# Five chunks held back for the third-stage stretch in a long convolution with a gated mix

## The chip, the cores and the metric

The kernel runs on one core of a Trainium2 chip. The time is device microseconds (us) of one launch. Five engines work side by side, each on its own queue of instructions, in the order in which they were written: TensorE (PE, matmuls; PEld is its weight load), VectorE (DVE), ScalarE (ACT), GpSimd (POOL), and SyncE (SP), which issues the DMAs here. An instruction waits at the head of its queue until what it needs is there, and everything behind it on that engine waits with it. Matmuls write to PSUM, which the kernel holds as a few buffers that are used in turn.

## The reference

```python
Xf = np.fft.rfft(x, n=2 * S, axis=1)           # x: 8 x 6400 x 128
Hf = np.fft.rfft(h, n=2 * S, axis=0)           # h: 6400 x 128
y = np.fft.irfft(Xf * Hf[None], n=2 * S, axis=1)[:, :S]
gate_pre[:, s] = sum_k conv_w[k] * y[:, s - 4 + k]     # 5 taps, zeros before the start
out = (1 / (1 + np.exp(-gate_pre)) * (y @ w_val)) @ w_out
```

A convolution as long as the sequence, per channel, through a transform; then a five-tap convolution along the sequence gives a gate for a projection, and the gated result is projected again. Everything is float32.

## The kernel before

The transform of length 6400 is split as 100 x 64 and done with matmuls by constant matrices, in four stages for each of the 8 batches.

- The *first stage* (`Forward`): GpSimd makes a difference and a sum of two halves of the input (`sums`, tiles `sd` from tiles `x`), PE multiplies them by the matrix `r1` (`half`), ScalarE copies the result into `gy`.
- The *second stage* (`Product`): for each of 13 blocks `kb`, PE multiplies `gy` by a block of the matrix `m2` that is loaded anew each time (three buffers); VectorE multiplies the result by the spectrum of `h`, in two instructions (`mul_u` writes back to `gy`, `mul_t` into the buffer of `h` itself), and GpSimd joins the two with two adds. The spectrum is loaded too, into four buffers `h`. Each of these loads is 512 KB.
- The *third stage* (`s3_quads`): 16 steps. PE multiplies `gy` by `r3` into a pair buffer of PSUM; ScalarE copies a part to one of the `h` buffers and writes the ends, VectorE makes two joins into the large tile `dt`.
- The *fourth stage* (`Chunk.s4`): 13 chunks of positions, twelve of five and one of four (`HEAD`, positions 60 to 63). PE multiplies a slice of `dt` by the resident matrix `m4`. ScalarE copies the chunk (`copies`: the values `y`, the initial value of the gate's cells, and a scaled copy `q` for one tap), VectorE adds the other taps in three instructions or a few more (`taps`), GpSimd adds `q`. Then PE projects `y` (`project`), ScalarE takes the sigmoid (`sigm`), VectorE multiplies (`gate`), PE projects again (`output`), ScalarE copies and SP stores (`store`).

The program alternates between two stretches. In the **third-stage stretch** of a batch each of the 16 steps holds one third-stage step and one half of the next batch's first stage, and after these some of the last batch's deferred work. In the **fourth-stage stretch** that follows, each step holds one chunk of the fourth stage, one product of the next batch, and the projections of earlier chunks. Five chunks, those at positions 35 to 55, are *late*: in the fourth stretch only their values are copied; their taps, gate and projections come in the next third stretch, two steps for each. They have tiles of their own (`yl`, and `gl` for the cells). All other chunks keep values and cells in `dt`.

The order is written out by hand: the dictionary `steps` places deferred work in the third stretch, `jobs` places projections in the fourth, and a wrapper keeps every engine in program order. PSUM has two pair buffers (third stage, products) and four single ones (first and fourth stage, projections). A chunk's single buffer is free when its taps have been read from it.

Of the kernel before, what the change touches and what calls it, by code (L numbers as in the profile page):

```python
# [36 lines left out]
DEFER = 35  # L37
# [4 lines left out]
XH = 8  # L42

# [78 lines left out]
def longconv_moe(ctx: ExitStack, tc: tile.TileContext, x, h, r1, m2, r3, m4, w64, out):  # L122
# [23 lines left out]
    m2_sb = [cp.tile([128, SB, 2, C], F32, name=f"m2_{i}") for i in range(M2B)]  # L146
    h_sb = [cp.tile([128, 2 * SB * C], F32, name=f"h_{i}") for i in range(HB)]
    x_sb = [cp.tile([128, 2, XG, N2], F32, name=f"x_{i}") for i in range(XB)]
    sd_sb = [cp.tile([128, 2, XG, N2], F32, name=f"sd_{i}") for i in range(3)]
    p_t = [cp.tile([128, CH, N1], F32, name=f"p_{i}") for i in range(2)]  # L150
    hd = dp.tile([NKB, 128, 2 * SB * C], F32, name="hd")
# [241 lines left out]
    def cells(x, n):  # L393

        out, i = [], 0
        while i < n:
            y = x + i
            end = 4 if y < 4 else LATE if y < LATE else N2
            k = min(n - i, end - y)
            s = (y - 4) % N2  # L400
            out.append((i, gl[:, y - LATE : y - LATE + k] if y >= LATE else dv[:, s : s + k, 1, :N1]))
            i += k
        return out

    class Chunk:


        def __init__(self, b, ch, defer):
            self.b, self.ch = b, ch
            a, n = ch  # L410
            self.late = defer and DEFER <= a < HEAD[0]
            self.y = yl[a][:, :n] if a >= LATE else dv[:, a : a + n, 0, :N1]
# [26 lines left out]
        def copies(self):  # L439
# [8 lines left out]
            else:  # L448
                act(self.y, self.p)
                if not self.late:  # L450
                    self.init()
                    self.q = p_t[a // CH % 2]
                    self.first(3, self.q, self.p)
            if self.late:
                self.p = self.y

# [5 lines left out]
        def taps(self, js=range(4)):  # L462
            a, n = self.ch
            if self.late and 0 in js:
                self.init()
                self.q = p_t[a // CH % 2]
                self.first(3, self.q, self.p)
# [15 lines left out]
            if 3 not in js:  # L483
                return
            for i, o in cells(a + 3, n):
# [68 lines left out]
    m4_rest = [12, 11, 10, 9, 4, 8, 5, 7, 6]  # L554
# [24 lines left out]
    for b in range(B):  # L579
# [4 lines left out]
        for m, c in enumerate(pend[1:]):  # L584
            steps[2 * m] += [lambda c=c: c.taps(range(2))]
            steps[2 * m + 1] += [lambda c=c: c.taps(range(2, 4))]
            steps[2 * m + 2] += [c.project, c.sigm, c.gate]
            if m < 3:
                steps[2 * m + 4] += [c.output]
                steps[2 * m + 5] += [c.store]  # L590
        if pend:
            steps[13] += [pend[0].project, pend[0].sigm, pend[0].gate]
# [3 lines left out]
        for g in range(NS):  # L596
# [14 lines left out]
            if nxt and g % 2 and g > 1:  # L611
                kb = g // 2 - 1
                if kb < M2B:
                    m2_load(kb)
                elif kb < M2B + HB - 1:
                    h_load(kb - M2B)
# [8 lines left out]
        cs = [Chunk(b, ch, nxt) for ch in CHUNKS]  # L625
        jobs = collections.defaultdict(list)
        for i, c in enumerate(cs):
            if i and not c.late:
                jobs[i + 2 if nxt else (5, 6, 7, 8, 9, 10, 11, 11, 12, 13, 13, 14)[i - 1]].append(c)
        if not nxt:  # L630
            jobs[NCH + 1].append(cs[0])
        ps, outs = {}, []
        for s in range(max(NCH - 1, *jobs) + 2):
            if s < 2:
                cs[s].s4()
            if s == 0 and pend:
                pend[0].output()
                pend[0].store(p_t[1][:, : HEAD[1]])
            if nxt and s == 0:
                ps[0] = Product(0)  # L640
                m2_load(M2B)
            if nxt and s + 1 < NKB:
                ps[s + 1] = Product(s + 1)
                m2_load(s + 1 + M2B)
# [6 lines left out]
            late = pend[4 + s : 5 + s] if s < 2 else []  # L651
# [66 lines left out]
```

## Time and profile before

| what | value |
|---|---|
| median of 3 runs (lowest to highest) | 1002.31 us (1001.48 to 1006.22) |
| profiled execution, its span | 1004.56 us, 1002.7 us |
| PE, DVE busy | 871.8 us (87%), 745.1 us (74%) |
| POOL, ACT busy | 570.1 us (57%), 509.6 us (51%) |
| moved by DMA | 177.40 MB, 177 GB/s on average |

Third- and fourth-stage stretches lie one behind the other from 97.6 us on; before that the spectrum of `h` is made and batch 0 goes through its first two stages. An average over the whole span mixes the two kinds of stretch, so the views are read stretch by stretch: from the first matmul of the third stage (`pt<-r_sb,gy`) to the first of the fourth (`pt<-m_sb,dt`) and on to the next batch's third. All program lines appear under the line of one helper, L109, so instructions are told apart by their tiles and shapes. In the rows, "pt" is a PSUM buffer, and the words in brackets say how long the engine was idle before and who ended the wait.

### The profile page before, as it was taken

What the parts mean: (1) busy time and instruction counts of PE and PEld (TensorE: products, weight loads), DVE (VectorE), ACT (ScalarE), POOL (GpSimd) and SP (SyncE); (2) the same over time, 40 slices, a digit from 0 to 9 for tenths busy, and PEclk for the clock granted to TensorE, in tenths of its full rate; (3) what the DMA queues carried; (4) which work ended last, traced back from release to release, by engine and by line L of the source; (5) the groups of instructions that cost most, each with busy time, mean ns of one, the idle gap of its engine ahead of it and who ended that gap; (6) DMA issues with size and microseconds to landing.
All of it is one profiled execution on the core that took longest, in us unless ns stands there. A gap on an engine that the chain in (4) does not pass through costs nothing. (4 is left out here: it accounts for less than half of the span.)

```text
span 1002.7 us, 47817 instructions
## 1 busy us (share of the span) xinstructions
PE 871.8 (87%) x21360; PEld 719.6 (72%) x21360; DVE 745.1 (74%) x1033; ACT 509.6 (51%) x1207; POOL 570.1 (57%) x586
## 2 busy tenths in 40 slices
PE   7898769988799879988899778988799888997778
PEld 6798668775688558775788657876688757884554
DVE  5556547968598767968499675968589675978666
ACT  4431444546553654547444663546544574545456
POOL 5457535775477754786277663776367762761032
PEclk9799879999999989999899999999899999999999
DMA  7684647846486456855486565855478454850103
GB/s 255 229 304 190 192 141 258 262 107 185 154 264 185 144 160 213 231 135 164 142 264 183 141 197 162 242 157 162 134 240 222 139 170 138 266 144 23 42 22 111
DMA packets 96844, 177.40 MB, mean 177 GB/s; under 512 B 43392, under 2 KB 49792, under 8 KB 96640
## 3 DMA queue, kind: packets, MB, share of 16 engines
q1 hardware_dynamic: 96640, 174.35, 56.2%
q8 instruction: 168, 2.75, 1.1%
q14 instruction: 36, 0.29, 0.1%
HBM read 141.56 MB, written 32.77 MB: 174 GB/s over the span
## 5 line engine op out<-in xcount | busy, mean ns | idle before, releaser
L109 POOL TENSOR_TENSOR gy<-gy,h 128x512 f32<-128x512 f32 (+1 forms) x182 | 221.2, 1242 | 120.1 <-PE pt L109 87.5
L109 PEld LDWEIGHTS pt<-r_sb,gy 64*64 64x64 f32 x8192 | 157.1, 145 | 103.6 <-issue 60.6
L109 DVE TENSOR_TENSOR dt<-pt,h 128x496 f32<-128x496 f32 x256 | 159.7, 664 | 96.2 <-ACT dt L109 91.8
L109 PEld LDWEIGHTS pt<-m_sb,dt 128*64 128x64 f32 x4096 | 194.0, 139 | 51.2 <-issue 34.2
L109 PE MATMUL pt<-r_sb,gy 64*64 64x64 f32 x8192 | 173.6, 233 | 60.1 <-issue 45.2
L109 PE MATMUL pt<-m_sb,dt 128*64 128x100 f32 x4096 | 200.2, 253 | 14.5 <-DVE dt L109 13.0
L109 POOL TENSOR_TENSOR sd<-x 128x256 f32<-128x256 f32 x236 | 182.0, 803 | 47.1 <-issue 21.2
L109 PEld LDWEIGHTS pt<-gy,m 128*64 128x64 f32 x3008 | 179.8, 135 | 27.7 <-issue 22.8
L109 PE MATMUL pt<-r_sb,sd 50*64 50x100 f32 x4608 | 155.0, 270 | 46.0 <-issue 21.0
L109 PE MATMUL pt<-gy,m 128*64 128x128 f32 x3008 | 190.8, 277 | 0.6 <-PE pt L109 0.5
L109 PEld LDWEIGHTS pt<-r_sb,sd 50*64 50x64 f32 x4608 | 128.6, 149 | 55.1 <-issue 24.2
L109 ACT COPY dt<-pt 128x16 f32<-128x16 f32 (+3 forms) x397 | 113.8, 329 | 103.6 <-PE pt L109 103.6
L109 DVE TENSOR_TENSOR gy<-pt,h 128x1024 f32<-128x1024 f32 (+1 forms) x99 | 116.7, 1179 | 58.3 <-ACT gl L109 34.4
L109 DVE SCALAR_TENSOR_TENSOR dt<-pt,w_sb,dt 128x500 f32<-128x500 f32 (+7 forms) x216 | 132.5, 629 | 10.6 <-POOL dt L109 6.7
L109 ACT COPY gy<-pt 128x400 f32<-128x400 f32 x248 | 112.2, 512 | 42.5 <-PE pt L109 31.2
L109 ACT COPY h<-pt 128x512 f32<-128x512 f32 (+1 forms) x136 | 83.5, 614 | 91.5 <-issue 43.0
L109 POOL TENSOR_TENSOR gl<-gl,p 128x500 f32<-128x500 f32 (+1 forms) x48 | 56.8, 1183 | 114.4 <-DVE gl L109 94.0
L109 PE MATMUL pt<-dt,w_sb 128*64 128x500 f32 (+2 forms) x480 | 115.1, 555 | 2.4 <-ACT dt L109 1.8
L109 DVE SCALAR_TENSOR_TENSOR gl<-yl,w_sb,gl 128x500 f32<-128x500 f32 (+1 forms) x112 | 106.1, 953 | 13.4 <-ACT gl L109 12.1
L109 DVE TENSOR_TENSOR h<-pt,h 128x1024 f32<-128x1024 f32 (+1 forms) x91 | 107.7, 1183 | 3.1
L109 ACT COPY yl<-pt 128x500 f32<-128x500 f32 (+1 forms) x89 | 51.3, 577 | 91.8 <-PE pt L109 91.7
L109 POOL TENSOR_TENSOR dt<-dt,p 128x500 f32<-128x500 f32 (+1 forms) x64 | 66.3, 1041 | 23.2 <-PE pt L109 13.2
(44 smaller groups left out, 657.6 us busy)
## 6 DMA issues: line engine op xcount, KB each, us to landing
m<-m SPq DMA_DIRECT2D x90, 512.0 KB, 5.4
h<-hd SPq DMA_DIRECT2D x84, 512.0 KB, 5.1
x<-xl SPq DMA_DIRECT2D x118, 256.0 KB, 2.9
out<-dt SPq DMA_DIRECT2D x56, 250.0 KB, 4.4
out<-yl SPq DMA_DIRECT2D x40, 250.0 KB, 4.6
m_sb<-m SPq DMA_DIRECT2D x12, 375.0 KB, 5.9
hd<-h SPq DMA_DIRECT2D x8, 512.0 KB, 4.9
m_sb<-m SPq DMA_DIRECT2D x6, 512.0 KB, 7.2
```

The costliest lines, as they stand in the source:

```text
L109: return self._tc.keep_in_program_order(call(*args, **kwargs))
```

## The change

The chunks at 10 to 30 become *held*: in the fourth stretch their taps are added as before, but their projection, sigmoid, gate and output come in the steps 0 to 6 of the next third stretch (stores up to step 7). The late chunks move back there by four steps, to steps 4 to 14, and one more of their outputs is done there instead of in the fourth stretch. To have a place until then, values and cells of positions 10 to 34 leave `dt` for a tile `ring`, which also takes the place of the three `m2` and four `h` buffers: in the first half of the fourth stretch it holds those, in the second the held chunks. So the products come earlier: two in even steps, one in odd ones, all 13 within nine steps. The fourth stage takes `HEAD`, 0, then the late chunks, then 5 to 30. The first loads of `m2` and `h` for the next batch stand at steps given by a table, `AHEAD`. GpSimd's add of `q` is taken out of `taps` and comes one step later, after the next chunk's taps; `q` then needs four buffers instead of two, and two of them are `sd` tiles. Cells of a chunk that crosses position 10 are two pieces instead of one. The five loads of `m4` blocks that are left for batch 0's fourth stretch come in another order, and its 17 steps in batch 7 follow the same rule, projection three steps behind the chunk.

```diff
-DEFER = 35
+HELD = 10
+BL = 2 * SB * C
+AHEAD = {2: (1, 0), 7: (0, 0), 9: (0, 1), 10: (0, 2), 11: (1, 1), 13: (1, 2)}
...
+    ring = cp.tile([128, (M2B + HB) * BL], F32, name="ring")
+    ring_at = [ring[:, i * BL : (i + 1) * BL] for i in range(M2B + HB)]
+    m2_sb = [r.rearrange("p (s a c) -> p s a c", a=2, c=C) for r in ring_at[:M2B]]
+    h_sb = [ring_at[M2B + i] for i in (2, 0, 1, 3)]
+    held_c = ring[:, : (LATE - HELD) * N1].rearrange("p (n t) -> p n t", t=N1)
...
+            self.held = defer and HELD <= a < LATE
+            self.y = yl[a][:, :n] if a >= LATE else held_y[a] if a >= HELD else dv[:, a : a + n, 0, :N1]
...
+        def keep(self):
+            self.q = p_t[self.i % 2] if self.late else keeps[self.i % 4]
+            self.first(3, self.q, self.p)
...
-            if 3 not in js:
-                return
-            for i, o in cells(a + 3, n):
+        def add(self):
+            for i, o in cells(self.ch[0] + 3, self.ch[1]):
                 nc.gpsimd.tensor_tensor(out=o, in0=o, in1=self.q[:, i : i + o.shape[1]], op=ADD)
...
+        for c in pend:
+            a = c.ch[0]
+            if a == HEAD[0]:
+                t = NS - 1
+            elif c.held:
+                t = (a - HELD) // CH
+            else:
+                t = 6 + 2 * (a - LATE) // CH
+                steps[t - 2] += [lambda c=c: c.taps(range(2))]
+                steps[t - 1] += [lambda c=c: c.taps(range(2, 4)), c.add]
+            steps[t] += [c.project, c.sigm, c.gate]
+            if t + 2 < NS:
+                steps[t + 2] += [c.output]
+                steps[t + 3] += [c.store]
...
+            kbs = list(range(at, min(at + 2 - s % 2, NKB))) if nxt else []
+            at += len(kbs)
             if s < 2:
                 cs[s].s4()
...
+            if s == 0:
+                s2(0)
+            for kb in kbs[:1]:
+                s2(kb + 1)
...
             if 1 < s < NCH:
                 cs[s].s4()
...
+            for kb in kbs[:1]:
+                times(kb)
+            for kb in kbs[1:]:
+                s2(kb + 1)
             if s < NCH:
                 cs[s].copies()
...
+            for kb in kbs[1:]:
+                times(kb)
             if 0 < s <= NCH and not cs[s - 1].late:
                 cs[s - 1].taps()
+            if 2 < s < NCH + 2 and not cs[s - 2].late:
+                cs[s - 2].add()
             for c in jobs[s]:
                 c.gate()
```

Here `s2(kb)` issues a product's matmuls and the load of the block of `m2` three further on, `times(kb)` the multiplications, the adds and the load of the block of `h` four further on.

PE, second half of a middle batch's fourth stretch, up to the first matmuls of the third stage (`pt<-r_sb,gy`). `m_sb,dt` is a chunk's fourth stage, `gy,m` or `gy,ring` a product, `dt,w_sb` a projection or an output. Before:

```order
L109 MATMUL pt_8198<-gy,m_1_81 64x64x2 x16
L109 MATMUL pt_8215<-dt,w_sb 64x500 x2
L109 MATMUL pt_8218<-m_sb,dt 64x2x50 x20
L109 MATMUL pt_8239<-dt,w_sb 64x500 x2
L109 MATMUL pt_8251<-gy,m_2_82 64x64x2 x16
L109 MATMUL pt_8268<-m_sb,dt 64x2x50 x20
L109 MATMUL pt_8289<-dt,w_sb 64x500 x2
L109 MATMUL pt_8302<-gy,m_0_80 64x64x2 x8
L109 MATMUL pt_8311<-m_sb,dt 64x2x50 x20
L109 MATMUL pt_8337<-m_sb,dt 64x2x50 x20
L109 MATMUL pt_8369<-r_sb,gy 64x64 x32
```

And now:

```order
L111 MATMUL pt_6340<-gy,ring 64x64x2 x8
L111 MATMUL pt_6349<-m_sb,dt 64x2x50 x20
L111 MATMUL pt_6378<-m_sb,dt 64x2x50 x20
L111 MATMUL pt_6411<-m_sb,dt 64x2x50 x20
L111 MATMUL pt_6440<-dt,w_sb 64x500 x2
L111 MATMUL pt_6443<-m_sb,dt 64x2x50 x20
L111 MATMUL pt_6476<-m_sb,dt 64x2x50 x20
L111 MATMUL pt_6497<-dt,w_sb 64x500 x2
L111 MATMUL pt_6509<-m_sb,dt 64x2x50 x20
L111 MATMUL pt_6552<-r_sb,gy 64x64 x32
```

The last product now stands six chunks ahead of the third stage, and of the projections only one chunk's are left there.

VectorE in the same place. `gy<-pt` and the row after it are a product, SCALAR_TENSOR_TENSOR are taps, `dt<-pt,h` or `dt<-pt,ring` the joins of the third stage. Before:

```order
L109 TENSOR_TENSOR dt<-pt_8215,dt 128x5x100
L109 TENSOR_TENSOR gy<-pt_8198,h_85 128x2x64x8
L109 TENSOR_TENSOR h_85<-pt_8198,h_85 128x1024
L109 TENSOR_TENSOR gy<-pt_8251,h_86 128x2x64x8
L109 TENSOR_TENSOR h_86<-pt_8251,h_86 128x1024
L109 TENSOR_TENSOR gy<-pt_8302,h_83 128x2x64x4
L109 TENSOR_TENSOR h_83<-pt_8302,h_83 128x512
L109 TENSOR_TENSOR dt<-pt_8369,h_86 128x124x4
```

And now:

```order
L111 SCALAR_TENSOR_TENSOR ring<-pt_6443,w_sb,ring 128x500 x3
L111 SCALAR_TENSOR_TENSOR ring<-pt_6476,w_sb,ring 128x500 x3
L111 SCALAR_TENSOR_TENSOR ring<-pt_6509,w_sb,ring 128x500
L111 SCALAR_TENSOR_TENSOR ring<-pt_6509,w_sb,ring 128x400
L111 SCALAR_TENSOR_TENSOR gl<-pt_6509,w_sb,gl 128x100
L111 SCALAR_TENSOR_TENSOR ring<-pt_6509,w_sb,ring 128x300
L111 SCALAR_TENSOR_TENSOR gl<-pt_6509,w_sb,gl 128x200
L111 TENSOR_TENSOR dt<-pt_6552,ring 128x124x4
L111 TENSOR_TENSOR dt<-pt_6552,ring 128x62x2x4
L111 TENSOR_TENSOR ring<-pt_6613,ring 128x500
```

Where products stood ahead of the first joins there are now taps, and the gate of a held chunk (the last row) stands behind the first two joins.

GpSimd in the same place. `gy<-gy` are a product's adds, `ring<-ring` and `gl<-gl` the adds of `q`, `sd<-x` the sums of the first stage. Before:

```order
L109 TENSOR_TENSOR gl<-gl,p_93 128x300
L109 TENSOR_TENSOR gy<-gy,h_84 128x64x8 x2
L109 TENSOR_TENSOR gy<-gy,h_85 128x64x8 x2
L109 TENSOR_TENSOR gy<-gy,h_86 128x64x8 x2
L109 TENSOR_TENSOR gy<-gy,h_83 128x64x4 x2
L109 TENSOR_TENSOR sd_90<-x_87 128x256 x2
```

And now:

```order
L111 TENSOR_TENSOR ring<-ring,sd_85 128x500
L111 TENSOR_TENSOR ring<-ring,p_87 128x500
L111 TENSOR_TENSOR ring<-ring,p_88 128x500
L111 TENSOR_TENSOR ring<-ring,sd_84 128x200
L111 TENSOR_TENSOR gl<-gl,sd_84 128x300
L111 TENSOR_TENSOR sd_84<-x_81 128x256 x2
```

The adds of the last held chunks now stand ahead of the first sums; the last product's adds are far ahead of them.

More of the change, by code (lines that the diff above doesn't have):

```diff
@@ L397, in cells @@
             y = x + i
-            end = 4 if y < 4 else LATE if y < LATE else N2
+            end = next(e for e in (4, HELD, LATE, N2) if y < e)
             k = min(n - i, end - y)
             s = (y - 4) % N2
-            out.append((i, gl[:, y - LATE : y - LATE + k] if y >= LATE else dv[:, s : s + k, 1, :N1]))
+            t, o = (gl, y - LATE) if y >= LATE else (held_c, y - HELD) if y >= HELD else (dv[:, :, 1, :N1], s)
+            out.append((i, t[:, o : o + k]))
             i += k
@@ L465, in taps @@
                 self.init()
-                self.q = p_t[a // CH % 2]
-                self.first(3, self.q, self.p)
+                self.keep()
             if a == HEAD[0]:
@@ L583, in longconv_moe @@
         steps = collections.defaultdict(list)
[L584 to L592, printed above, removed]
+        for c in pend:
[12 more added lines that the diff above has]
+                steps[t + 3] += [c.store]
+        pend = [c for c in pend if c.ch[0] in (HEAD[0], HEAD[0] - CH)]
         if nxt:
@@ L610, in longconv_moe @@
                     m4_load(m4_rest.pop(0))
[L611 to L616, printed above, removed]
+            if nxt and g in AHEAD:
+                f, kb = AHEAD[g]
+                (h_load if f else m2_load)(kb)
             for u in steps[g]:
@@ L622, in longconv_moe, with s2, times @@
             fx = Forward(x[b + 2], gy)
-        cs = [Chunk(b, ch, nxt) for ch in CHUNKS]
+        chs = CHUNKS if not nxt else sorted(CHUNKS, key=lambda c: (c != HEAD, c[0] > 0, c[0] < LATE))
+        cs = [Chunk(b, i, ch, nxt) for i, ch in enumerate(chs)]
         jobs = collections.defaultdict(list)
         for i, c in enumerate(cs):
-            if i and not c.late:
-                jobs[i + 2 if nxt else (5, 6, 7, 8, 9, 10, 11, 11, 12, 13, 13, 14)[i - 1]].append(c)
+            if i and not c.late and not c.held:
+                jobs[i + 3].append(c)
         if not nxt:
-            jobs[NCH + 1].append(cs[0])
-        ps, outs = {}, []
-        for s in range(max(NCH - 1, *jobs) + 2):
+            jobs[NCH + 2].append(cs[0])
+        pr = {}
+        def s2(kb):
+            if nxt and kb < NKB:
+                pr[kb] = Product(kb)
+                m2_load(kb + M2B)
+        def times(kb):
+            if kb in pr:
+                pr[kb].mul_u()
+                pr[kb].mul_t()
+                pr.pop(kb).add()
+                h_load(kb + HB)
+        outs, at = [], 0
+        for s in range(max(NCH, *jobs) + 2):
+            kbs = list(range(at, min(at + 2 - s % 2, NKB))) if nxt else []
+            at += len(kbs)
             if s < 2:
                 cs[s].s4()
[L636 to L644, printed above, removed]
+            late = pend[s : s + 1]
+            if late and s == 0:
+                late[0].output()
+                late[0].store(p_t[1][:, : HEAD[1]])
+                late = []
+            if s == 0:
+                s2(0)
+            for kb in kbs[:1]:
+                s2(kb + 1)
             if m4_rest:
@@ L671, in longconv_moe @@
                 fx.load(XB)
-        pend = [cs[0]] + [c for c in cs if c.late]
+        pend = [cs[0]] + [c for c in cs if c.held or c.late]
 def _lay_x(v):
```

25 lines of the change are left out of this document (10 added, 15 removed).

## The prediction

> **What bounds the kernel now.** I read the page's busy shares first, then the windows of the alternating stretches (columns: window, its length, then busy time and instruction count of PE, PEld, DVE, ACT, POOL; granted clock; DMA share; GB/s). The third-stage stretch of batch 0 starts at 97.6, its fourth-stage stretch at 153.4, and so on to the two of batch 7.
>
> ```profile
> PE 871.8 (87%) x21360; PEld 719.6 (72%) x21360; DVE 745.1 (74%) x1033; ACT 509.6 (51%) x1207; POOL 570.1 (57%) x586
> ...
> 97.60:153.40 55.80, 37.93 (x1536) 36.38 (x1537) 30.17 (x55) 25.30 (x80) 24.10 (x33) 0.80 0.46 150
> ...
> 265.20:324.50 59.30, 59.26 (x984) 50.63 (x984) 51.19 (x66) 25.70 (x47) 40.50 (x36) 1.00 0.74 217
> 324.50:380.80 56.30, 43.92 (x1576) 32.81 (x1573) 38.45 (x54) 34.55 (x100) 30.98 (x37) 0.91 0.46 143
> ...
> 840.40:899.70 59.30, 59.30 (x988) 50.59 (x988) 51.18 (x66) 25.71 (x47) 40.51 (x36) 1.00 0.70 213
> 899.70:942.10 42.40, 28.84 (x1064) 20.07 (x1062) 33.66 (x54) 21.92 (x68) 6.24 (x5) 1.00 0.06 22
> 942.10:1002.70 60.60, 50.87 (x632) 32.38 (x632) 37.22 (x62) 36.76 (x70) 15.46 (x15) 0.94 0.22 67
> ```
>
> A fourth-stage stretch is PE's: 59.26 busy of 59.30, VectorE close behind with 51.2. A third-stage stretch belongs to no engine: PE 43.9 and VectorE 38.5 of 56.3. One period (fourth stretch, then the next batch's third) takes (840.4 − 153.4) / 6 = 114.5 us. The timeline shows how a third stretch starts and how the fourth after it does:
>
> ```profile
> 324.55 1.19 PE L109 MATMUL pt<-r_sb,gy 64*64 64x64 f32 x64
> 326.96 0.92 PE L109 MATMUL pt<-r_sb,sd 50*64 50x100 f32 x32 [1.23 <-POOL sd L109]
> 327.70 1.14 PE L109 MATMUL pt<-r_sb,gy 64*64 64x64 f32 x64
> ...
> 329.35 1.14 PE L109 MATMUL pt<-r_sb,gy 64*64 64x64 f32 x64
> ...
> 380.82 1.59 PE L109 MATMUL pt<-m_sb,dt 128*64 128x100 f32 x32 [0.55 <-DVE dt L109]
> ...
> 385.04 1.22 DVE L109 TENSOR_TENSOR gy<-pt,h 128x1024 f32<-128x1024 f32 x1 [4.37 <-ACT gl L109]
> ```
>
> Step 0 already waits 1.23 us for GpSimd's sums (sd), so step 1 starts 3.15 after step 0. A step that nothing holds takes PE 1.65 (327.70 to 329.35). VectorE's first product comes 4.2 after the fourth stretch begins (380.82 to 385.04).
>
> **The change, part by part.** Prices are start-to-start times in one step of a fourth stretch:
>
> ```profile
> 404.15 2.28 DVE L109 SCALAR_TENSOR_TENSOR dt<-pt,w_sb,dt 128x500 f32<-128x500 f32 x3
> ...
> 405.06 2.01 PE L109 MATMUL pt<-gy,m 128*64 128x128 f32 x32
> ...
> 406.35 0.67 DVE L109 TENSOR_TENSOR dt<-pt,dt 128x500 f32<-128x500 f32 x1
> ...
> 406.86 1.26 POOL L109 TENSOR_TENSOR dt<-dt,p 128x500 f32<-128x500 f32 x1
> 406.90 1.01 PE L109 MATMUL pt<-dt,w_sb 128*64 128x500 f32 x4
> 406.93 1.21 DVE L109 TENSOR_TENSOR gy<-pt,h 128x1024 f32<-128x1024 f32 x1
> ...
> 407.74 1.89 PE L109 MATMUL pt<-m_sb,dt 128*64 128x100 f32 x40
> ...
> 408.18 1.22 DVE L109 TENSOR_TENSOR h<-pt,h 128x1024 f32<-128x1024 f32 x1
> ...
> 409.32 2.28 DVE L109 SCALAR_TENSOR_TENSOR dt<-pt,w_sb,dt 128x500 f32<-128x500 f32 x3
> ...
> 409.47 1.00 PE L109 MATMUL pt<-dt,w_sb 128*64 128x500 f32 x4
> 409.53 2.52 POOL L109 TENSOR_TENSOR gy<-gy,h 128x512 f32<-128x512 f32 x2 [1.42 <-PE pt L109]
> ```
>
> PE: a product 1.84 (405.06 to 406.90), a projection or an output about 0.8 (406.90 to 407.74), a chunk's fourth stage 1.73. VectorE: a product 2.4 (406.93 to 409.32), a chunk's taps 2.2 (404.15 to 406.35), a gate 0.6. GpSimd: a product's two adds 2.52, a chunk's add 1.26.
>
> *Leaving the fourth stretch*: five projections, five outputs and one late output (of the chunk at 50), 11 × 0.8 = 8.8 us of PE, and five gates of 0.67, 3.4 us of VectorE. Cell ranges now also break at position 10, which adds two short taps (+0.6). So PE needs 59.3 − 8.8 = 50.5 and VectorE 51.2 − 3.4 + 0.6 = 48.4. If all of it vanished into PE's idle time of the third stretch, 8.8 a period would be won. I choose otherwise, because the order is no longer mixed: thirteen products stand in the first nine steps and six chunks' taps behind them, with no product beside them.
>
> *The fourth stretch.* VectorE waits 4.2 for its first product. In steps 5, 6 and 7 the next product's matmuls (1.84) stand on PE behind a chunk's fourth stage (1.73), once also behind an output; with two pair buffers VectorE waits about 1.2 in each, 3.5 in all, and some 1.4 in the tail (the gate of the chunk at 5 behind its late add and sigmoid). Its last tap ends at 4.2 + 48.4 + 4.9 = 57.5 after the stretch began. PE has only 10 us of matmuls beside those last 14.7 us of taps (6 × 2.25 and a gate) and reaches the first quads of the third stage at about 53.
>
> *The add one block behind.* The add of a chunk now waits for the next chunk's taps, so the last two (chunks at 25 and 30; the latter in two pieces) run after the last tap: about 2.5. Only then come the sums that the forward stage wants, on the same queue.
>
> ```profile
> L109 POOL TENSOR_TENSOR sd<-x 128x256 f32<-128x256 f32 x236 | 182.0, 803 | 47.1 <-issue 21.2
> ```
>
> Two of 0.80: the first forward half starts at 57.5 + 2.5 + 1.6 = 61.6, and with it (0.7) and the held projection (0.8) step 1 starts at 63.1. Before, it started at 59.3 + 3.15 = 62.5. What PE saved is given back as one idle gap, 54 to 61.6; queued behind it are step 1's quads, and VectorE stands with the gate of the chunk at 10 ahead of step 1's joins.
>
> *The third stretch.* Steps 1 to 3 have no late taps: PE's 1.65 plus 0.8, 1.6 and 1.6 of held work, 8.9; VectorE (two joins, a gate) and ScalarE have less. A gap costs the clock besides. The rows are two PE gaps and windows at and after them:
>
> ```profile
> 366.04 1.86 PE L109 MATMUL pt<-r_sb,gy 64*64 64x64 f32 x57 [2.19 <-issue]
> ...
> 372.04 0.64 PE L109 MATMUL pt<-r_sb,gy 64*64 64x64 f32 x26 [2.11 <-issue]
> ...
> 365.00:369.00 4.00, 2.96 (x93) 2.96 (x97) 1.11 (x3) 1.20 (x5) 2.52 (x4) 0.63 0.76 264
> ...
> 373.00:377.00 4.00, 4.00 (x103) 2.53 (x100) 1.83 (x3) 1.87 (x6) 0.00 (x0) 0.59 0.02 4
> ```
>
> After such a gap the granted clock was 0.63 and 0.59 over 4 us: 1.5 us of PE time lost. For a gap of 7.6 I take 2.0 (bounds 0 and two such windows, 3.0). The Trainium skill ("TensorE: Matmul & The Clock Gate", Part 1, the HAM clock gate) says the array drops to half rate after an idle window of about 3.4 us and returns after a busy one. By that rule the gap surely spans a window, and half rate lasts 3.4 to 6.8 us, 1.7 to 3.4 of PE time; the trace shows the drop after shorter gaps than the rule asks.
>
> Steps 4 and 5 hold the first late chunk. From its add on, pairs of steps follow one another in a closed chain:
>
> ```profile
> 570.29 1.26 POOL L109 TENSOR_TENSOR gl<-gl,p 128x500 f32<-128x500 f32 x1 [2.49 <-DVE gl L109]
> ...
> 572.84 2.43 DVE L109 SCALAR_TENSOR_TENSOR gl<-yl,w_sb,gl 128x500 f32<-128x500 f32 x2
> ...
> 575.19 1.24 DVE L109 TENSOR_TENSOR dt<-pt,h 128x496 f32<-128x496 f32 x2
> ...
> 577.23 1.26 POOL L109 TENSOR_TENSOR gl<-gl,p 128x500 f32<-128x500 f32 x1 [2.49 <-PE pt L109]
> ```
>
> Add, sigmoid, gate, two taps, joins, tap, add: 6.94 a pair. The change leaves that chain as it is: four pairs, 27.8. Up to the first add, steps 4 and 5 take quads 1.1, ScalarE's copies about 1.1, joins 1.24, the held gate 0.67, and 4.4 from the two taps to the add (572.84 to 577.23): 8.5, and I add 0.7 for an issue gap. The held outputs and stores (up to step 7) lie in its slack. Two steps remain after the last add, 55.8 / 16 = 3.5 each (batch 0's stretch, which has no late work).
>
> *Sum of a period*: 63.1 + 8.9 + 2.0 + 8.5 + 0.7 + 27.8 + 7.0 = 118.0, against 114.5: +3.5, six times, +21.
>
> *The other stretches.* Batch 0 loads five blocks of constants (375 KB each, 1.9 MB) in the first steps, beside products that now come two to a step. What loads cost, and the fastest 4 us of them:
>
> ```profile
> m<-m SPq DMA_DIRECT2D x90, 512.0 KB, 5.4
> h<-hd SPq DMA_DIRECT2D x84, 512.0 KB, 5.1
> ...
> 277.00:281.00 4.00, 4.00 (x85) 4.00 (x82) 3.96 (x9) 1.02 (x3) 2.33 (x3) 1.00 1.02 358
> ```
>
> At 358 GB/s the blocks take 5.3; I charge 2, since not every load is late (bounds 0 and 5.3). In the other batches a product needs two of these loads, 1.05 MB or 2.9 us at that rate, where products come every 3.0 us on average: just covered. An h buffer turns round in a product (2.4), its adds (2.52) and a landing (5.1), 10.0 for four products: covered as well.
>
> Batch 7 has no forward stage, so no sums are waited for; its third stretch is the late chain alone, 6.0 a pair (first two rows, of the chain of waits). Its fourth stretch runs taps, add, taps, add in series, 3.74 a chunk (last two rows):
>
> ```profile
> 906.36 1.26 POOL gl L109
> ...
> 912.37 1.25 POOL gl L109
> ```
>
> ```profile
> 961.62 2.29 DVE L109 SCALAR_TENSOR_TENSOR dt<-pt,w_sb,dt 128x500 f32<-128x500 f32 x3 [1.45 <-POOL dt L109]
> ...
> 965.36 2.29 DVE L109 SCALAR_TENSOR_TENSOR dt<-pt,w_sb,dt 128x500 f32<-128x500 f32 x3 [0.80 <-POOL dt L109]
> ```
>
> From the start of batch 6's fourth stretch: last tap at 57.5, four steps of joins (1.24) and gate (0.67) to 65.1, the first chain to its add 5.2, four pairs 24.0, two steps 4.5: 98.8, against 59.3 + 42.4 = 101.7, so −3. In the last stretch the add leaves the taps' way; PE is next, 1.73 + 0.8 + 0.8 = 3.3 a chunk, 12 × 0.4 = −5.
>
> *Sum*: +21 + 2 − 3 − 5 = +15. The profiled execution took 1004.56, 1.9 of it outside its span of 1002.7; that is 0.2% above the median of the runs shown, 1002.31. A difference of spans carries over, and I predict 1002.3 + 15 = **1017 us**, slower.
>
> **The rivals.**
>
> *The steps run free* (0.27). In the kernel before, the steps behind the late pairs are slow because PE gaps put down to "issue" recur there (2.19 and 2.11 above). With no such gaps and no clock loss the period is 63.1 + 8.9 + 8.5 + 27.8 + 4.9 (two steps of 1.65 with two pieces of 0.8) = 113.2, −1.3, and the time 1002.3 − 8 + 2 − 8 = 988. For it: held work spreads PE's instructions, and fewer steps run bare. Against it: the gaps are in every stretch with forward work, batch 0's included. The Trainium skill ("Runtime: NRT & Kernel Launch", Instruction fetch mechanics) has instructions streamed in 16 KiB blocks with the cost mostly hidden. By that rule the two steps would take 4.9 and the sum would come 6 × 2.1 lower, 1004; the 2 us gaps of this trace do not look hidden.
>
> *PE's 8.8 us vanish in idle time* (0.05): 7 × 8.8 = 62 less, 941. For it: 12 us of PE idle in each third stretch. Against it: VectorE's 48.4 plus its start is already 52.6, and the gap at the sums.
>
> *The gap costs no clock, and steps 4 and 5 meet no issue gap* (0.18): 118.0 − 2.0 − 0.7 = 115.3, +0.8 a period, and the time 1002.3 + 5 + 2 − 8 = 1001, no change. For it: after step 0's wait of 1.23 the next steps follow 1.65 apart, at full speed (327.70, 329.35). Against it: 7.6 is six times that wait.
>
> *Loads set the pace of the crowded products* (0.07): at 358 GB/s a product's loads take 2.9; with stores between them, and 217 GB/s being what the whole stretch had before, 3.4 a product is possible, 13 × 0.4 = 5 more a period, half of it covered by VectorE's own waits: 7 × 2.5 = 18 more, 1035. It decides once a landing exceeds about 6.5 instead of 5.1.
>
> **How the numbers follow.** My forecast has 0.43, the rivals 0.27, 0.05, 0.18 and 0.07. Faster by over 0.5% (about what a measurement of this kernel tells from none) are the first two, 0.32; within it 0.18; slower 0.50. The range holds forecast, first, third and fourth rival: from 982, a free run with a gap 1 us shorter in six periods, to 1036. The forecast's own range, with the bounds of clock (0 to 3.0), constants and two steps, is 1005 to 1028.
>
> **What would show it.** In a middle fourth stretch PE falls well below 100% busy, and VectorE is busy to its end. At each start of a third stretch PE waits some 7 us for GpSimd's sums, where it was 1.2, with the granted clock at half behind it. The late pairs still take 6.9. The last fourth stretch shows no VectorE waits on GpSimd and is some 5 us shorter. I am wrong if the first forward half comes less than 2 us after the first quads, if steps 1 to 3 take much less or more than 9 to 11 together, or if products wait for loads of h or m.

## The result and the profile after

The changed kernel took 1030.9 us (median of 4 runs, 1027.35 to 1034.45); the kernel before took 1003.6 beside it. The ratio is 1.0271, 95% interval 1.0214 to 1.0328: slower by 2.7%, where 1.5% was forecast. The profiled execution took 1034.45 us, its span is 1032.6. The page's busy shares hardly moved, and the windows of the stretches (columns as in the prediction) show where the time went:

```profile
PE 874.2 (85%) x21360; PEld 700.7 (68%) x21360; DVE 744.7 (72%) x1049; ACT 505.1 (49%) x1215; POOL 563.4 (55%) x594
```

```profile
152.30:206.90 54.60, 50.30 (x933) 46.65 (x933) 44.83 (x56) 18.48 (x33) 35.87 (x33) 1.00 0.68 239
393.50:448.30 54.80, 51.38 (x941) 47.67 (x941) 45.23 (x57) 18.43 (x35) 35.88 (x33) 1.00 0.65 216
448.30:516.70 68.40, 54.92 (x1618) 35.82 (x1616) 44.05 (x67) 41.73 (x114) 34.39 (x42) 0.88 0.42 133
...
876.20:930.80 54.60, 51.16 (x940) 47.33 (x940) 45.21 (x57) 18.46 (x35) 35.82 (x33) 1.00 0.60 203
930.80:978.60 47.80, 37.41 (x1110) 21.93 (x1107) 40.44 (x67) 28.62 (x82) 10.96 (x10) 1.00 0.15 52
978.60:1032.60 54.00, 46.76 (x628) 29.76 (x628) 37.68 (x65) 36.21 (x70) 15.54 (x16) 0.99 0.22 75
```

A fourth stretch fell from 59.9 us (mean of batches 0 to 5 before) to 54.8, and PE is no longer busy all through it. The third stretch behind it rose from 54.6 to 65.9. A period went from 114.5 to (876.2 − 152.3) / 6 = 120.65. Against the spans of before: six periods +37.0, batch 6's fourth with batch 7's third stretch +0.6, the last fourth stretch −6.6, everything up to batch 0's fourth stretch −1.1; together +29.9, the difference of 1032.6 and 1002.7.

The timeline of the start of batch 3's third stretch shows the price of the new order on GpSimd:

```profile
448.30 1.19 PE L111 MATMUL pt<-r_sb,gy 64*64 64x64 f32 x64
...
452.53 1.24 POOL L111 TENSOR_TENSOR ring<-ring,p 128x500 f32<-128x500 f32 x1 [1.00 <-issue]
452.65 1.24 DVE L111 TENSOR_TENSOR dt<-pt,ring 128x496 f32<-128x496 f32 x2
453.73 0.60 POOL L111 TENSOR_TENSOR ring<-ring,sd 128x200 f32<-128x200 f32 x1
454.29 0.81 POOL L111 TENSOR_TENSOR gl<-gl,sd 128x300 f32<-128x300 f32 x1
455.19 4.14 POOL L111 TENSOR_TENSOR sd<-x 128x256 f32<-128x256 f32 x6
...
456.64 1.61 PE L111 MATMUL pt<-r_sb,sd 50*64 50x100 f32 x32 [7.16 <-POOL sd L111]
...
458.18 1.94 PE L111 MATMUL pt<-ring,w_sb 128*64 128x500 f32 x4
...
460.05 1.70 PE L111 MATMUL pt<-r_sb,gy 64*64 64x64 f32 x64
461.57 0.86 PE L111 MATMUL pt<-r_sb,sd 50*64 50x100 f32 x32
```

VectorE's last tap ends as the joins begin (452.65), 59.2 after the fourth stretch's start at 393.5. Three pieces of add follow on GpSimd, then the sums; PE waits 7.16 us and runs its next four projection matmuls in 1.94 us; the granted clock in the trace is 0.5 from 454.43 to 461.26. The waits of PE, summed from batch 0's fourth stretch to batch 6's, before and after (total, times, longest):

```profile
PE pt L109 <- issue: 45.4, 38, 2.7
PE pt L109 <- POOL sd L109: 10.5, 9, 2.3
```

```profile
PE pt L111 <- POOL sd L111: 42.9, 6, 7.2
PE pt L111 <- issue: 29.5, 21, 3.3
...
PE pt L111 <- DMA ring<-m: 0.6, 2, 0.4
```

Six gaps of 7.15 us, one in each middle period. There are fewer issue gaps than before, but they now lie elsewhere. The late adds on GpSimd and PE's rows between two of them, batch 3 (the worst period; over the six, the four late pairs have a mean of 30.7 us, 28.4 to 34.4; before 28.4, 28.2 to 28.9):

```profile
478.38 1.25 POOL L111 TENSOR_TENSOR gl<-gl,p 128x500 f32<-128x500 f32 x1 [4.28 <-DVE gl L111]
...
485.55 1.25 POOL L111 TENSOR_TENSOR gl<-gl,p 128x500 f32<-128x500 f32 x1 [2.72 <-ACT dt L111]
...
493.83 1.24 POOL L111 TENSOR_TENSOR gl<-gl,p 128x500 f32<-128x500 f32 x1 [3.84 <-ACT dt L111]
...
505.16 1.25 POOL L111 TENSOR_TENSOR gl<-gl,p 128x500 f32<-128x500 f32 x1 [6.83 <-ACT dt L111]
```

```profile
485.23 1.06 PE L111 MATMUL pt<-gl,w_sb 128*64 128x500 f32 x4
...
490.47 0.40 PE L111 MATMUL pt<-r_sb,gy 64*64 64x64 f32 x10 [2.35 <-issue]
...
495.84 0.93 PE L111 MATMUL pt<-r_sb,sd 50*64 50x100 f32 x12 [2.05 <-issue]
496.70 1.94 PE L111 MATMUL pt<-gl,w_sb 128*64 128x500 f32 x4
```

In the kernel before the first late add came 9.5 us after the third stretch's start, the last at about 38, and 16.7 us of steps without late work followed, where most issue gaps fell. Now the first comes at 30.0 and the last at 60.8 of 65.9, and the gaps at steps 9 to 14 fall between the late adds, where nothing hides them.

### The profile page after: what moved, and what is told of

It is laid out like the page before. It is cut to its first block, busy times and chain, and to the rows that moved or that the text cites. A ratio compares the mean times of both kernels' runs of the same rounds, so it can differ in the third digit from the quotient of the medians.

```text
span 1032.6 us, 47904 instructions
## 1 busy us (share of the span) xinstructions
PE 874.2 (85%) x21360; PEld 700.7 (68%) x21360; DVE 744.7 (72%) x1049; ACT 505.1 (49%) x1215; POOL 563.4 (55%) x594
## 4 chain that ended last, share of the span: by engine, by line
PE 54%; DVE 12%; issue 9%; ACT 5%; POOL 3%; DMA 1%; DVEq 0%; SPq 0%; ACTq 0%; POOLq 0%
PE pt L111 54%; DVE ring L111 5%; DVE dt L111 4%; DVE gy L111 2%; ACT ring L111 2%; DVE gl L111 2%; DMA ring<-m 1%; POOL gl L111 1%; ACT gl L111 1%; ACT p L111 1%; POOL sd L111 1%; ACT dt L111 1%; POOL ring L111 1%; POOL gy L111 0%; ACT sd L111 0%
## 5 line engine op out<-in xcount | busy, mean ns | idle before, releaser
L111 POOL TENSOR_TENSOR gy<-gy,ring 128x512 f32<-128x512 f32 (+1 forms) x182 | 220.2, 1242 | 122.5 <-DVE ring L111 77.2
L111 DVE TENSOR_TENSOR dt<-pt,ring 128x496 f32<-128x496 f32 x256 | 160.1, 667 | 78.7 <-ACT dt L111 78.3
L111 PE MATMUL pt<-r_sb,sd 50*64 50x100 f32 x4608 | 150.9, 270 | 72.2 <-POOL sd L111 42.9
L111 PE MATMUL pt<-m_sb,dt 128*64 128x100 f32 x4096 | 193.8, 249 | 14.5 <-DVE dt L111 6.7
L111 ACT COPY ring<-pt 128x512 f32<-128x512 f32 (+2 forms) x216 | 129.4, 603 | 145.0 <-PE pt L111 86.7
L111 PE MATMUL pt<-gy,ring 128*64 128x128 f32 x3008 | 188.5, 278 | 12.8 <-PE pt L111 10.3
L111 PEld LDWEIGHTS pt<-gy,ring 128*64 128x64 f32 x3008 | 176.0, 135 | 21.6 <-PE pt L111 17.9
L111 DVE TENSOR_TENSOR ring<-pt,ring 128x1024 f32<-128x1024 f32 (+2 forms) x131 | 134.8, 1029 | 51.8 <-PE pt L111 41.4
L111 DVE TENSOR_TENSOR gy<-pt,ring 128x1024 f32<-128x1024 f32 (+1 forms) x99 | 116.8, 1180 | 67.3 <-PE pt L111 63.7
L111 POOL TENSOR_TENSOR gl<-gl,p 128x500 f32<-128x500 f32 (+1 forms) x38 | 47.1, 1238 | 143.5 <-DVE gl L111 111.9
L111 ACT COPY dt<-pt 128x16 f32<-128x16 f32 (+3 forms) x317 | 67.4, 265 | 105.0 <-PE pt L111 104.9
L111 DVE SCALAR_TENSOR_TENSOR ring<-pt,w_sb,ring 128x500 f32<-128x500 f32 (+4 forms) x136 | 91.8, 675 | 9.0 <-ACT sd L111 1.7
L111 PE MATMUL pt<-ring,w_sb 128*64 128x500 f32 x320 | 84.9, 632 | 1.5 <-DVE ring L111 1.4
```

The lines of the kernel that those rows point to most:

```text
L111: return self._tc.keep_in_program_order(call(*args, **kwargs))
```

## The experiments

Theory A is the prediction's: VectorE's taps end the fourth stretch, the sums behind the last adds leave PE a gap, and a late chain that starts later shows all that is put before it. Its rivals are named in the expectations. The kernel before was run again beside each group of runs (999.3 with e1 to e4, 1002.4 with e5 to e8, 1003.3 with e9 and e10), so ratios compare better than microseconds. "Period" is the one defined above, from the profiled execution alone, which lies up to 6 us from the median (e1: 993.2 against 987.4), so a difference of under 1 us a period is not told from none.

| kernel | us (median) | ratio to before, 95% interval | period, us |
|---|---|---|---|
| changed kernel | 1030.9 | 1.0271 (1.0214 to 1.0328) | 120.65 |
| e1 sums first | 987.4 | 0.9891 (0.9851 to 0.9930) | 113.8 |
| e2 add at once | 1072.0 | 1.0741 (1.0696 to 1.0787) | 124.4 |
| e3 none held | 1043.5 | 1.0426 (1.0375 to 1.0478) | 121.55 |
| e4 gap filled | 1029.4 | 1.0307 (1.0268 to 1.0346) | 120.0 |
| e5 = e1 without six loads | 974.5 | 0.9717 (0.9651 to 0.9782) | 110.4 |
| e6 = e1, loads earlier | 991.6 | 0.9893 (0.9823 to 0.9962) | 113.4 |
| e7 = e1, late chunks earlier | 990.5 | 0.9876 (0.9839 to 0.9913) | 114.3 |
| e8 = e1, product first | 981.4 | 0.9794 (0.9734 to 0.9854) | 112.0 |
| e9 = e8, loads in halves | 980.3 | 0.9771 (0.9729 to 0.9813) | 111.9 |
| e10 = changed, without six loads | 1017.1 | 1.0140 (1.0091 to 1.0190) | 117.6 |

### e1: the sums ahead of the last adds

```diff
+            if s == 12 and b + 2 < B:
+                for _ in range(2):
+                    fx.sums(nc.gpsimd)
             if 2 < s < NCH + 2 and not cs[s - 2].late:
                 cs[s - 2].add()
...
-        if nxt:
+        if nxt and b == 0:
             for _ in range(2):
                 fx.sums(nc.gpsimd)
```

The buffers of `q` were changed with it, since the sums now write `sd` while the last chunks still wait for their adds.

> Edit: in the middle batches the first two sums of the next batch's forward stage are issued to GpSimd before the last two adds of the fourth stretch instead of behind them; everything else stays. Theory A (the gap): TensorE's 7.15 us gap at step 0 of each middle third stretch comes from GpSimd being late, and the half clock of some 1.9 us behind it comes from the gap. A expects the gap to shrink to 1 to 2 us, step 0 to take about 5 us instead of 11.7, the first late add some 7 us earlier than 30 us after the stretch's start, each middle period 6 to 8 us shorter than 120.6, and 975 to 995 us in all. Theory B (the holding): the late chain is long because the held projections stand in front of it, and a free GpSimd only moves the wait; B expects the period within 2 us of 120.6 and 1020 to 1035 us.

The period fell by 6.9 us, and the kernel is 1.1% faster than the one before. The timeline of the same place (batch 3, third stretch from 434.39):

```profile
434.39 1.19 PE L111 MATMUL pt<-r_sb,gy 64*64 64x64 f32 x64
...
435.18 2.78 POOL L111 TENSOR_TENSOR sd<-x 128x256 f32<-128x256 f32 x4
...
436.63 0.92 PE L111 MATMUL pt<-r_sb,sd 50*64 50x100 f32 x32 [1.05 <-POOL sd L111]
...
437.92 2.47 POOL L111 TENSOR_TENSOR ring<-ring 128x500 f32<-128x500 f32 x2
...
438.47 1.21 PE L111 MATMUL pt<-r_sb,gy 64*64 64x64 f32 x64
```

The gap is 1.05 us instead of 7.16, step 0 takes 4.1 instead of 11.7, and the first late add comes at 23.0 instead of 30.0. The late pairs stay at a mean of 30.8. So the gap, which comes from the queue order on GpSimd and not from the amount of work, accounts for all of the period's loss against before (6.2) and a little more. Theory B is ruled out.

### e2: the add directly behind the taps

```diff
-            if 2 < s < NCH + 2 and not cs[s - 2].late:
-                cs[s - 2].add()
+                if s > 1:
+                    cs[s - 1].add()
```

> Edit: GpSimd's add of a chunk is issued directly behind that chunk's taps again, in every batch; the holding, the order and the loads stay as changed. Theory A (the add one block behind is a gain in the chain of taps and adds, and only its last piece is in the way): the chunks share cells, so taps and adds run serially again; the last fourth stretch goes from 54 back to 59 to 61 us, the middle fourth stretches grow by 4 to 7 us each, and the whole comes to 1050 to 1080 us. Theory C (the add one block behind is itself what costs, through the gap at step 0): the gap at step 0 falls to under 3 us, the middle periods shrink by 5 us or more, and the whole comes below 1010 us.

A's numbers came for the whole and for the last fourth stretch, which is back at 60.0. A period is 3.8 us longer than the changed kernel's; the middle fourth stretches grew by 2.8 (54.8 to 57.6), less than A's 4 to 7. The gap at step 0 didn't shrink, it is 7.7 to 9.3. VectorE's waits on GpSimd in the last fourth stretch, in the kernel before and here:

```profile
DVE dt L109 <- POOL dt L109: 6.7, 6, 1.5
```

```profile
DVE ring L111 <- POOL ring L111: 4.7, 5, 1.3
```

In the changed kernel no wait of VectorE's in that stretch is on GpSimd; without the add one block behind they return. The add one block behind is a gain by itself. Theory C is ruled out.

### e3: nothing held

```diff
-            self.held = defer and HELD <= a < LATE
+            self.held = False
...
-                t = 6 + 2 * (a - LATE) // CH
+                t = 2 + 2 * (a - LATE) // CH
...
-        pend = [c for c in pend if c.ch[0] in (HEAD[0], HEAD[0] - CH)]
+        pend = [c for c in pend if c.ch[0] == HEAD[0]]
```

> Edit: no chunk is held; the five chunks are projected in the fourth stretch as the others are, and the late chunks start at step 0 of the third stretch, four steps earlier than in the changed kernel. The order of the fourth stretch, the second stage ahead, the place of the loads and the add one block behind stay. Theory A (the gap and the late start of the chain each cost, and the holding buys nothing in the fourth stretch because VectorE bounds it there): the first late add falls from 30 us after the stretch's start to about 15 to 18 us, the tail grows by 6 to 12 us, the fourth stretches grow by 3 to 6 us because TensorE has the projections back, and the whole comes to 995 to 1012 us. Theory C (the add one block behind costs, whatever is held): it stays at 1020 us or above.

Neither theory describes what came. The time is on C's side, but the gap at the sums is gone; A's time is missed by over 30 us. The windows of batch 2's fourth and batch 3's third stretch:

```profile
395.50:461.60 66.10, 59.99 (x979) 49.43 (x977) 52.70 (x69) 24.68 (x47) 42.77 (x41) 1.00 0.55 187
461.60:515.90 54.30, 42.46 (x1582) 32.17 (x1581) 36.73 (x53) 35.56 (x101) 27.44 (x34) 0.97 0.50 158
```

The first late add comes at 7.4 and the third stretch is back at 54.9 (mean), but the fourth is 66.7, not the 58 to 61 that A gave it. The new order without holding is 7.1 us a period slower than the kernel before; holding gives back 11.9 in the fourth stretch and takes 11.0 of it in the third. So holding, with the late chain four steps later, is worth about 1 us a period in these profiles, and 1.5% of the whole by the ratios (1.0426 against 1.0271); my sentence that it buys nothing in the fourth stretch was wrong: without it that stretch is bound by neither engine (PE 60.0 and VectorE 52.7 of 66.1). That the projections, gates and outputs of the last chunks then trail behind the last tap (which ends at 61.4) fits these rows, but no run tests it by itself.

### e4: the gap filled with matmuls

```diff
-                f = fx.half([single(), single()])
+                pts = [single(), single()]
+                for k in range(17 if b and g == 0 else 0):
+                    o = slice(k % 2 * HP, (k % 2 + 1) * HP)
+                    nc.tensor.matmul(pts[0][o, :500], lhsT=w_sb[:, o], rhs=m4_flat[:, :500], start=True, stop=True)
+                f = fx.half(pts)
```

> Edit: 17 matmuls of 500 columns, whose results are overwritten, are added on TensorE at step 0 of the third stretch from the second batch on, so that TensorE doesn't idle while it waits for GpSimd's sums; nothing else changes. Theory A: the matmuls behind the gap run at 0.42 us instead of 0.88 us, step 0 becomes some 1.9 us shorter, each middle period 1.5 to 2 us, and the whole comes to 1015 to 1024 us. Theory D (the clock behind the gap costs nothing, since VectorE or GpSimd bounds these steps): the whole stays at 1028 to 1034 us, or above if the added matmuls delay the first forward half.

```profile
445.95 1.19 PE L111 MATMUL pt<-r_sb,gy 64*64 64x64 f32 x64
447.07 7.76 PE L111 MATMUL pt<-m_sb,w_sb 128*64 128x500 f32 x34
454.76 0.92 PE L111 MATMUL pt<-r_sb,sd 50*64 50x100 f32 x32
455.61 1.06 PE L111 MATMUL pt<-ring,w_sb 128*64 128x500 f32 x4
456.60 1.19 PE L111 MATMUL pt<-r_sb,gy 64*64 64x64 f32 x64
457.61 0.87 PE L111 MATMUL pt<-r_sb,sd 50*64 50x100 f32 x32
```

The four projection matmuls take 1.06 us instead of 1.94: the slow matmuls behind the gap come from PE's having stood idle. The slow clock ends inside step 1's quads, so its price is read up to the forward half behind them: from the first forward half to the second it is 2.85 us (454.76 to 457.61), in the changed kernel 4.93 (456.64 to 461.57). The clock costs 2.08 a gap. The added matmuls hold the first half up by 0.47, so 1.6 should be gained; the first late add comes 1.2 earlier (mean 28.9). But the late pairs came out at 31.4 instead of 30.7, and the period gained only 0.6. The expected 1015 to 1024 was missed. The whole lies where theory D put it, but not for D's reason: the clock does cost, and most of what is won is lost again behind it, within what the issue gaps add or leave out from one period to the next. The Trainium skill ("TensorE: Matmul & The Clock Gate", Part 1: The HAM clock gate) gives half rate after an idle window of about 3.4 us until a busy one has passed, from which the prediction estimated 1.7 to 3.4 us of PE time. The 2.08 measured here agrees with that estimate.

### e5 and e10: the loads left out

On e1 (e5) and on the changed kernel itself (e10):

```diff
-            if nxt and g in AHEAD:
+            if nxt and b == 0 and g in AHEAD:
```

> Edit, on top of the kernel with the sums first (e1): from batch 1 on, the six loads of the second stage's first blocks (512 KB each) that stand in steps 2 to 13 of the third stretch are left out, so that part of the second stage computes with old data; the same instructions run. Theory E (these loads hold up TensorE's instructions, and that makes the issue gaps in the late pairs): issue gaps over 0.6 us in steps 6 to 15 mostly vanish, the four late pairs go from a mean of 30.8 us to 28.4, the two steps behind them shrink by about 1 us, each period by 2 to 4 us, and the whole comes to 963 to 976 us. Theory F (the gaps come with TensorE's dense small matmuls, whatever the queues carry): the pairs stay at 29.5 to 31.5 us and the whole at 982 to 992 us.

> Edit, on the changed kernel itself: from batch 1 on the six loads in steps 2 to 13 of the third stretch are left out, so that part of the second stage computes with old data; the sums stay where the change has them. Theory E (the late pairs are longer than forecast because these loads hold up TensorE's instructions): the four late pairs go from a mean of 30.7 us to 28.5, the two steps behind them from 5.2 to 4, the gap of 7.15 us and the first late add at 30.0 us stay, each period gets 3 to 3.5 us shorter, and the whole comes to 1008 to 1014 us. If the pairs were long for another reason (the late start itself, or the clock after the gap), they stay above 30 us and the whole at 1025 us or more.

Theory E holds in both. PE's waits over the six periods, e1 and then e5:

```profile
PE pt L111 <- issue: 34.4, 25, 3.5
```

```profile
PE pt L111 <- issue: 12.3, 16, 2.0
```

And e10, with batch 3's late adds:

```profile
PE pt L111 <- POOL sd L111: 42.9, 6, 7.2
...
PE pt L111 <- issue: 10.3, 16, 1.8
```

```profile
472.47 1.25 POOL L111 TENSOR_TENSOR gl<-gl,p 128x500 f32<-128x500 f32 x1 [4.29 <-DVE gl L111]
...
479.42 1.26 POOL L111 TENSOR_TENSOR gl<-gl,p 128x500 f32<-128x500 f32 x1 [2.49 <-ACT dt L111]
```

Without the loads the pairs are 6.95 apart again, four of them take 28.6 (e5) and 28.55 (e10) in the mean, and the two steps behind them 4.0 in every period. The period loses 3.4 and 3.1 us. The six gaps of 7.15 at the sums are untouched in e10 (42.9, as in the changed kernel), so the two losses are separate. e10's whole, 1017.1, lies 3 us above the expected 1008 to 1014: its period fell by the lower end of what was given.

### e6 and e9: the loads moved, and cut

e6 is e1 with the first edit; e9 is e8 with five loads cut in halves, the second:

```diff
-AHEAD = {2: (1, 0), 7: (0, 0), 9: (0, 1), 10: (0, 2), 11: (1, 1), 13: (1, 2)}
+AHEAD = {2: (1, 0), 5: (0, 0), 7: (0, 1), 8: (0, 2), 9: (1, 1), 10: (1, 2)}
```

```diff
-                (h_load if f else m2_load)(kb)
...
+                    nc.sync.dma_start(h_sb[kb % HB][:, o], hd[kb, :, o])
+                else:
+                    k = SB // 2 * (1 - g % 2)
+                    nc.sync.dma_start(m2_sb[kb][:, k : k + SB // 2], m2[:, kb * SB + k : kb * SB + k + SB // 2])
```

> Edit, on top of e1: the same loads, with five of the six at steps 5, 7, 8, 9 and 10 instead of 7, 9, 10, 11 and 13. Theory E (loads cause issue gaps): the gaps move from steps 9 to 14 to steps 5 to 10; steps 5 to 8 are bound by TensorE and the late chain as the others are, so the whole stays within 5 us of e1's 987. Theory F (the gaps don't come from loads): nothing moves, 983 to 991 us. The run tells them apart by the place of the gaps, not by the time.

> Edit, on top of the kernel with the sums and the product first (e8): five of the six loads of the second stage's first blocks are cut in two halves of 256 KB, one in each step from 5 to 14, instead of whole ones of 512 KB at steps 7, 9, 10, 11 and 13; the bytes are the same. Theory E1 (a whole load's burst in front of TensorE's instructions makes the issue gaps, so shorter bursts make shorter gaps): the issue gaps of a middle third stretch fall from 4.7 us to 2 to 3.5, the period by 1 to 2.5 us, and the whole comes to 965 to 977 us. Theory E2 (the bytes count, not the burst): gaps and time stay, 978 to 986 us.

In e6 the issue gaps over 0.6 us of the six middle third stretches are 21, as in e1. In steps 5 to 10 they rose from 9 to 14, in steps 11 to 14 they fell from 12 to 7: some moved with the loads, not all, and the time stayed. In e9 they sum to 5.0 us a stretch, against 4.7 in e8, and the time didn't move: halves in twice as many steps delay PE as much, which is E2's side. So the size of one load is not what counts; that it is the bytes alone, as E2 has it, no run shows.

### e7 and e8: two tries for a faster kernel

e7 starts the late chunks two steps earlier (first edit), e8 issues the first product ahead of the fourth stretch's first chunks (second):

```diff
-                t = 6 + 2 * (a - LATE) // CH
+                t = 4 + 2 * (a - LATE) // CH
...
-        pend = [c for c in pend if c.ch[0] in (HEAD[0], HEAD[0] - CH)]
+        pend = [c for c in pend if c.ch[0] == HEAD[0]]
```

```diff
+            if s == 0:
+                s2(0)
             if s < 2:
                 cs[s].s4()
...
-            if s == 0:
-                s2(0)
```

> Edit, on top of e1: the five late chunks start two steps earlier in the third stretch (taps at steps 2 and 3, first late add at about 15.5 us instead of 23), beside the held work, and the chunk at 55 is put out in the third stretch too. Theory A (time from the start to the first late add, plus four pairs of about 7 us, plus free steps sets the stretch): steps 2 to 5 grow to about 4.4 us each, two free steps of 1.7 to 3.5 us come behind the last pair, and each period gets 1 to 3 us shorter, 966 to 981 us in all. Theory G (TensorE's issue gaps fill whatever is freed, as in the free steps of the kernel before): within 4 us of 987.

> Edit, on top of e1: the first product of the second stage is issued ahead of the fourth stretch's first chunks on TensorE instead of behind two chunks and a late output. Theory A (VectorE's chain from its first product to its last tap sets the fourth stretch's end): VectorE's first product starts 2 to 2.5 us after the stretch's start instead of 4.4, its last tap comes 1.5 to 2 us earlier, each period gets 1.5 to 2 us shorter, and the whole comes to 974 to 979 us. Theory H (the first matmuls of the stretch only change places, and TensorE or the loads set the pace of the products): within 3 us of 987.

e7: the first late add came at 15.8, as expected, and the gain was lost behind the last: four steps took 13.2 us there, 3.3 each, where two had taken 5.2. That is theory G's number, and half of the 32 us of issue gaps over 0.6 us in the six middle third stretches now fall in those last steps. e8: the period fell by 1.8, within A's 1.5 to 2; the whole is 2 us above its range, and 6 us below e1's by the medians. VectorE's waits from the fourth stretch's start to the last tap, changed kernel and e8 (batch 2 of each):

```profile
DVE gy L111 <- PE pt L111: 7.4, 4, 3.9
```

```profile
DVE gy L111 <- PE pt L111: 6.0, 5, 1.4
```

The first wait of 3.9 us is gone, the longest that is left is 1.4, and the sum fell by 1.4. Counted from the last first- or third-stage matmul, the first product comes 2.6 us earlier than in e1 and the last tap 1.2 (mean of six), a little less than expected. So VectorE's row of products and taps does set the end of the fourth stretch, and half of the time won at its head is lost again in later waits. With e9, 0.9771 (0.9729 to 0.9813), this is the fastest of the kernels that do the whole work; e8's interval overlaps with e9's.

## Why the prediction was right in its direction and short in its size

*The fourth stretch.* Right in kind: PE fell to 51.4 of 54.8 and VectorE works to the end. The last tap came at 59.2, not 57.5. The forecast was 48.4 busy and 9.1 of waits; measured were 49.3 busy, 8.2 of waits (3.94 for the first product and 1.06, 1.39 and 1.01 later, as expected, and 0.8 for ScalarE), and 1.7 in 26 short pauses between VectorE's instructions, which the sum left out.

*The add one block behind and the sums.* Right: 2.5 and 1.6 were given, and the half starts 3.9 after the last tap (456.64 − 452.7). The wait of 7.16 stands where 7.6 was forecast.

*The third stretch up to the first late add.* Given from the first half: 0.7 + 0.8 + 8.9 + 2.0 + 8.5 + 0.7 = 21.6; measured 21.7 (456.64 to 478.38). Inside it the clock took 2.08 (e4), where 2.0 was given.

*The four late pairs.* **This is the step that failed in its size.** "The change leaves that chain as it is: four pairs, 27.8": the chain is unchanged, but its time is not, 30.7. Of the 2.9 missing, 0.7 was there to be read: the last of the four pairs takes 7.4 to 7.6 in the kernel before too, where the four have a mean of 28.4. The rest comes with the loads: e10, without them, has 28.55. Loads as such don't lengthen the chain. In the kernel before, one load of 512 KB stood beside each pair, also where I read the 6.94 (SyncE's rows, batch 4):

```profile
568.21 0.42 SPq L109 DMA_DIRECT2D m<-m  x1
...
575.14 0.43 SPq L109 DMA_DIRECT2D m<-m  x1
```

In that kernel eight issue gaps over 0.6 us fell between the first and the last late adds of the six middle third stretches, 10.4 us in all, and the chain hid them. A pair has some 2 us to spare for PE (an estimate: 6.94 less two steps of 1.65 and two pieces of 0.8). In the changed kernel five loads stand beside the four pairs, three of them within 3 to 8 us; sixteen such gaps fall there, 27.3 us in all, some longer than the spare time. Whether the same loads spaced as before would be hidden again, no run shows. The two steps behind them were priced too high for a related reason: 3.5 each came from batch 0's stretch, with its gaps; measured 5.1 for both, and 4.0 without the loads.

*The sum of a period.* 118.0 forecast: +1.5 at the first half, +0.1 to the late add, +2.9 for the pairs, −1.85 for the last steps, 120.65. Six times 2.65 is 16; with the two parts below (+3.6 for batch 7's third stretch, −1.6 and −3.1 for the rest) these are the 14.9 us between +15 and the +29.9 of the spans, and they put the measured time above the forecast's own range of 1005 to 1028. That e10 comes to 1017, the forecast, is partly such cancelling and not a proof of each term.

*Batch 7's third stretch.* −3 was given, +0.6 measured. I let VectorE's joins and gate, 1.9 a step, set steps 0 to 3. From step 2 on PE sets them:

```profile
936.58 1.22 PE L111 MATMUL pt<-r_sb,gy 64*64 64x64 f32 x64 [1.45 <-DVE dt L111]
937.73 1.90 PE L111 MATMUL pt<-ring,w_sb 128*64 128x500 f32 x8
939.56 1.19 PE L111 MATMUL pt<-r_sb,gy 64*64 64x64 f32 x64
```

Quads of 1.15 and eight matmuls of held work of 1.83 make 2.98 a step. From the last tap to the first late add it took 14.5 us instead of 12.8 (7.6 and 5.2), so 1.7 of the 3.6 comes from here; 1.6 is the later last tap, as in the other batches, and 0.8 the pairs (24.8 instead of 24.0), less 0.5 for the last two steps. The numbers for PE's price were in the prediction; I used them for the middle batches and forgot them here.

*The rest.* The last fourth stretch gained 6.6 (5 given), and e2 shows that it is the add. Batch 0's fourth stretch is as long as the others (54.6): the constants cost nothing that shows, where 2 was charged.

*The rivals.* "The steps run free" was right about the two steps behind the late pairs: no issue gap over 0.6 us falls there any more, and they take 5.1, where it gave 4.9 and I gave 7.0. It fell as a whole, since the gaps now lie between the late adds. "The gap costs no clock" fell: 2.08 us. The issue waits are 10.3 us in six periods without the loads (e10) and 29.5 with them. The rule of the Trainium skill ("Runtime: NRT & Kernel Launch", Instruction fetch mechanics) that was set beside the first rival, instruction blocks streamed at a mostly hidden cost, agrees with the first number better than with the second. "PE's 8.8 us vanish in idle time" fell: e3 shows that what holding takes out of the fourth stretch comes back in the third. Loads did set a pace, but not the one of that rival: PE waits 0.6 us in all for data of m.

## What to carry to other kernels

When work is moved off an engine, look at which queue then ends last and what stands behind it: here two sums of 0.8 us behind the last adds cost 7 us a period, and putting them two adds earlier turned a loss of 2.7% into a gain of 1.1%. A chain's price holds for the place where it was read; if the chain moves under other work, count the loads that stand beside it in both places, and price each step by the slowest of its engines.

## What the runs showed of the hardware that was not expected

- **Loads hold up TensorE's instructions.** With six loads of 512 KB a period PE waits 29.5 us in six periods that are put down to "issue"; without them 10.3 stay (changed kernel and e10; e1 and e5: 34.4 and 12.3). The page lists a queue of instructions beside the loads' (the row below: packets, MB, share of 16 engines), with packets of 16 KB, and the trace has the time of each. In the six middle third stretches of every kernel here, every issue wait of PE over 0.6 us (28 in the kernel before, 16 in the changed one, 6 in e10) ends 1.2 to 1.6 us after the end of such a packet, and counted along PE's own instructions these waits lie at multiples of 256 from one another, give or take one. So PE waits there for its next block of instructions. The packets take as long with the loads as without (1.11 us in e1, 1.12 in e5), but they start later: after PE passes a block's end, the next packet starts over 2 us behind it in 21 of 70 cases in the changed kernel and in 2 of 68 in e10. Why they start late, no row shows. The Trainium skill ("DMA: Bandwidth & Descriptors", Queues, rings and completion order) says that a DMA engine turns to another queue only between whole packets. No run here shows which queue a DMA engine served.

```profile
q8 instruction: 168, 2.75, 1.1%
```

- **Half clock after one gap of 2.35 us.** PE waited 2.35 us up to 490.47 (row above) and then worked; the granted clock fell to 0.5 at 491.98, before the second wait (2.05 us, up to 495.84), and stayed there until 502.22. Four projection matmuls took 1.94 us in it (496.70), where four had taken 1.06 (485.23). In the 3.4 us up to the fall PE was busy for 1.5. The Trainium skill ("TensorE: Matmul & The Clock Gate", Part 1: The HAM clock gate) asks for an idle window of about 3.4 us. The wait here was shorter, and the clock fell all the same.
